# Convolution operations tied in the plan to the pace of the feed-forward items

## The chip, the cores and the metric

The kernel runs on one core of one Trainium2 chip. The metric is the device time of one execution in microseconds (us). Engines are called as in the profile: PE (TensorE), DVE (VectorE), ACT (ScalarE), POOL (GpSimd) and SP (SyncE, which here issues DMA).

## What is computed

A dynamic convolution over 2 x 4096 tokens of width 192, and behind it two feed-forward layers of width 2048, all in float32:

```python
w = softmax(weight_gen)                    # per token and head: 7 taps
x = sum over k of w[..., k] * x_shifted[k] # 8 heads of 24 columns, 6 tokens back
h = x @ w_in1;  g = where(h >= 1, h, where(h <= -1, 0, (h + 1)**2 / 4))
x = g @ w_out1                             # layer 1
h = x @ w_in2;  g = h - tanh(h)
out = g @ w_out2                           # layer 2
```

## The kernel before

The 8192 tokens are cut into 16 blocks of 512. A block goes through the convolution once and through layer 1 (m = 0) and layer 2 (m = 1). In a layer the hidden width of 2048 is 16 slices of 128; one slice of one block in one layer is an **item** (m, b, f). The order of the 512 items is written down in `order`: blocks 0 to 2 at the start in a mixed way, and then in turn 16 items of layer 1 of block b and 16 of layer 2 of block b - 1. Such 32 items are called a cycle here, 16 of them half a cycle. `at` gives an item's place.

An item (`item`) runs in this way. PE multiplies the block's columns with a slice of w_in into a PSUM bank. ACT and DVE make g of it: in layer 1 two ACT steps (L787, L788) and one of DVE (L789), in layer 2 one ACT step (L791) and one of DVE (L792). To keep float32 accuracy, g is split: ACT casts the high part gh (L793), DVE subtracts to get the low part gl (L797). PE multiplies gh and gl with a slice of w_out into two accumulator banks. At the end of a block `finish1` (layer 1, lines 844 to 856) or `finish2` (layer 2: an ACT copy at L877, DVE at L878 to L880, then 24 stores on SP's queue) takes the accumulators away.

From layer 1 of block 4 and layer 2 of block 3 on, two items run as a pair (`both`): matmuls of 64 rows, two at a time on the two halves of the array, 38 to a pair. A pair has three parts: `one` makes most of the first projection of its two items and the rest of the second projection of older ones, `two` reads gh and gl of the later item of the pair before the last, `three` those of the earlier item of the last pair.

The convolution of a block (`conv`) is a softmax of five short DVE steps and one of ACT, then 7 multiplications (L437) and 6 additions (L484, the last of them L573) over 128 x 768 values on DVE. For blocks 4 to 15 `move_rows` then splits the sum into a high and a low part (ACT L574, DVE L576), turns both (DVE L568, twice), sends them to DRAM and reads them back as columns. That makes 16 large DVE operations for a block.

The order of work on each engine is not written by hand. `Plan.add` takes a task with its engines and assumed durations, a key, the tasks that it depends on, and the buffers that it takes. `Plan.run` plays through these durations: whenever an engine is free it starts the ready task with the lowest key. What comes out is one fixed row of instructions for each engine, and only that reaches the chip, where an instruction waits for its data and for the instructions ahead of it in its row. An item's tasks have its place as key. A convolution's tasks begin at `base`, 36 places ahead of its block (40 for block 3), and go up by 1.1; but as they are started whenever nothing with a lower key is ready, they run far ahead of their keys, up to the number of buffers.

Of the kernel before, what the change touches and what calls it, by code (L numbers as in the profile page):

```python
# [14 lines left out]
ALU = mybir.AluOpType  # L15
AX = mybir.AxisListType
# [7 lines left out]
MOVED = 4  # L24
# [133 lines left out]
def on(engine, dur):  # L158
    return {engine: (dur, 0.0)}
# [3 lines left out]
def tile_dynconv_moe_moe(  # L163
# [86 lines left out]
    plan = Plan()  # L250
# [23 lines left out]
    order = []  # L274
# [96 lines left out]
    def conv(b, banks, base, gap):  # L371
# [4 lines left out]
        spare = slot("xt") if early else None  # L376
        j0 = b * T
        n0 = max(0, PAD - j0)
        count = [0]

        def key():
            count[0] += 1
            return base + gap * count[0]

        def load_wg(e):
            e.dma_start(wgs[wg.n].rearrange("p j h k -> p j (h k)"), wg_pj[:, b * T:(b + 1) * T, :])
# [18 lines left out]
        def bc(t):  # L405
            return t.unsqueeze(3).to_broadcast([P, T, H, K])
# [14 lines left out]
        lh = plan.add(on("DMA", 0.42 * n0), base - lead, load_halo, takes=[xw], late=2.0) if n0 else None  # L421
        lx = plan.add(on("DMA", 0.42 * (T + PAD - n0)), base - lead, load_x, takes=[] if n0 else [xw], uses=[xw] if n0 else [], late=2.0)
        whole = lambda k: lh if k + T <= n0 else lx
        t = plan.add(on("DVE", 0.30), key(), lambda e: e.tensor_reduce(MX(), W(), axis=AX.X, op=ALU.max), [lw], takes=soft, uses=[wg], own=0.12 if early else 0.0)
        t = plan.add(on("DVE", 0.30), key(), lambda e: e.tensor_tensor(W(), W(), bc(MX()), op=ALU.subtract), [t], uses=[wg] + soft, lock=not early)
        t = plan.add(on("ACT", 0.30), key(), lambda e: e.activation(W(), W(), AF.Exp), [t], uses=[wg])
        t = plan.add(on("DVE", 0.30), key(), lambda e: e.tensor_reduce(SM(), W(), axis=AX.X, op=ALU.add), [t], uses=[wg] + soft, own=0.12 if early else 0.0)

        def inverse(e):
            e.tensor_scalar(SM(), SM(), 1e-9, None, ALU.add)  # L430
            e.reciprocal(SM(), SM())

        t = plan.add(on("DVE", 0.47), key(), inverse, [t], uses=[wg] + soft, late=0.05, own=0.12 if early else 0.0)
        ts = plan.add(on("DVE", 0.30), key(), lambda e: e.tensor_tensor(W(), W(), bc(SM()), op=ALU.mult), [t], uses=[wg] + soft, lock=not early)

        def tap(e, dst, w, k):
            e.tensor_tensor(  # L437
# [53 lines left out]
        for fn, k, kind in tasks:  # L491
            last = early and k == mine - 1
            t = plan.add(
                on("DVE", 0.87), key(), fn, dep + [whole(k), lh], takes=([] if kind or k else [mem] + (area2 if b == 0 else [])),
                uses=([] if kind else [wg, xw]) + (more if kind or k or b else area) + ([mem] if kind or k else []),
                late=0.1, own=0.12 if early and b and (k if kind == 0 else last) else 0.0, lock=not early,
            )
            dep = [t]
# [5 lines left out]
            dep = [plan.add(on("DVE", 0.87), key(), lambda e: e.tensor_tensor(end, end, pool_mem(0), op=ALU.add), dep + [pa], uses=more + [spare], own=0.12)]  # L504

        if b >= MOVED:
            move_rows(b, wg, xw, mem, xt, dep, key)
            return

        def last_sum(e):  # L510
# [45 lines left out]
        marks["evac", b] = l1  # L556
        xdone[0, b] = [h0, h1, l0, l1]

    def move_rows(b, wg, xw, mem, xt, dep, key):
# [12 lines left out]

        t = plan.add(on("DVE", 0.87), key(), lambda e: e.tensor_tensor(acc_sb, acc_sb, prod_sb, op=ALU.add), dep, uses=[mem], lock=True)  # L573
        th = plan.add(on("ACT", 0.72), key(), lambda e: e.copy(hi_sb, acc_sb), [t], uses=[mem])  # L574
        tq = plan.add(on("DVE", 0.87), key(), lambda e: squares(e, 0, prod_sb), [th], uses=[mem, xw])
        tl = plan.add(on("DVE", 0.87), key(), lambda e: e.tensor_tensor(acc_sb, acc_sb, prod_sb, op=ALU.subtract), [th], uses=[mem], lock=True)  # L576
        tr = plan.add(on("DVE", 0.87), key(), lambda e: squares(e, 1, acc_sb), [tl, tq], uses=[mem, xw])
# [128 lines left out]
    def done(g, t):  # L706

        if g in late2 and late2[g][2] == NF - 1:
            m, b, f, *_, acc, need = late2[g]
            (finish1 if m == 0 else finish2)(b, acc, g + 7.0, t)  # L710

    def both(m, b, f, h0, h1, need):

# [22 lines left out]

        opens = [s for g in (g0, g1) if late2[g][2] == 0 for s in late2[g][8]]
        rest = lambda g: [s for s in used(g) if s not in opens]
        t = plan.add(on("PE", 2.08), i, one, need + [last[0]], takes=[h0, h1], uses=[xs, x3_of[m, b]] + used(o0, o1), late=0.0)
        done(o0, t)  # L740
        mid = plan.add(on("PE", 1.155), i, two, [t] + late2[g0][9], takes=[s for s in opens if s in late2[g0][8]], uses=[h0, xs] + used(o1) + rest(g0), late=0.35)
        done(o1, mid)
        end = last[0] = plan.add(on("PE", 1.155), i + 1, three, [mid] + late2[g1][9], takes=[s for s in opens if s in late2[g1][8]], uses=[h1, xs, x3_of[m, b]] + rest(g1), late=0.35)
        prev2[late2[g1][:2]] = end
        return mid, end

# [13 lines left out]
    def item(m, b, f, after):  # L760
# [178 lines left out]
UNTIL = 3.5  # L939
SKEW = 12  # L940
SKEW2 = 12
BASE3, BASE = 40.0, 36.0
LEAD = (4.0, 6.0)
CONV1 = (0.0, 0.35)
CONV2 = (14.0, 0.6)
# [29 lines left out]
```

## Time and profile before

| | |
|---|---|
| median of 3 runs | 1201.31 us (1200.46 to 1201.41) |
| the profiled execution | 1199.51 us, its span 1197.7 us |
| PE | busy 1151.5 us, 96% of the span |
| DVE | busy 994.1 us, 83% |
| ACT | busy 849.1 us, 71% |
| POOL | busy 98.6 us, 8%, all near the start |

The span is from the first to the last instruction of that one execution. Busy shares are means over stages: the start, with the weights being split into high and low parts, until about 225 us; whole-height items until 295 us; pairs until 1151 us; then the last half block. PE's records overlap, since the end of a matmul is modelled, so a busy PE can still be fed late.

### The profile page before, as it was taken

How to read it: one execution, taken by the hardware profiler on the slowest of the kernel's cores; microseconds unless marked ns; L12 is line 12 of the kernel's file. 1: busy time of each engine (PE TensorE's matmuls, PEld its weight loads, DVE VectorE, ACT ScalarE, POOL GpSimd, SP SyncE). 2: the span in 40 equal slices, each digit the busy share in tenths (PEclk: the TensorE clock that was granted, in tenths of full speed). 3: DMA queues.
4: the chain of work that ended last, by engine and by line, in shares of the span. 5: the costliest groups of instructions: out<-in, count | busy, mean ns of one | idle time of the engine just before them, and what ended most of it. 6: DMA issues, size and time to landing. Idle time of an engine off the chain costs nothing.

```text
span 1197.7 us, 23410 instructions
## 1 busy us (share of the span) xinstructions
PE 1151.5 (96%) x8648; PEld 1034.3 (86%) x8648; DVE 994.1 (83%) x1519; ACT 849.1 (71%) x1511; POOL 98.6 (8%) x85
## 2 busy tenths in 40 slices
PE   3899999999999999999999999999999999999998
PEld 2578778888788898999989899898999999999987
DVE  8999998999999989698796978779666666666665
ACT  4989896675767768677675766757677676867653
POOL 4743650000000000000000000000000000000000
PEclk9999999999999999999999999999999999999999
DMA  7422130232230213003030210302011010100000
GB/s 212 150 70 78 53 119 6 53 83 77 77 95 11 70 34 100 10 15 95 1 108 1 62 47 7 99 1 71 2 18 55 6 41 1 45 1 15 1 9 19
DMA packets 93034, 60.50 MB, mean 51 GB/s; under 512 B 56060, under 2 KB 81274, under 8 KB 92920
## 3 DMA queue, kind: packets, MB, share of 16 engines
q1 hardware_dynamic: 92732, 58.62, 17.4%
q8 instruction: 68, 1.11, 0.4%
q10 hardware_dynamic: 188, 0.39, 0.1%
q14 instruction: 46, 0.38, 0.1%
HBM read 43.24 MB, written 15.73 MB: 49 GB/s over the span
## 4 chain that ended last, share of the span: by engine, by line
PE 76%; DVE 14%; issue 4%; ACT 3%; DMA 2%; POOL 0%; SPq 0%; DVEq 0%; ACTq 0%; POOLq 0%
PE ps L669 33%; PE ps L685 29%; PE ps L773 7%; DVE gl L797 3%; DVE g L789 3%; DVE acc L484 1%; PE ps L814 1%; PE ps L808 1%; DVE prod L437 1%; PE ps L815 1%; PE ps L809 1%; PE ps L810 1%; PE ps L825 1%; DVE g L792 1%; ACT gh L793 1%
## 5 line engine op out<-in xcount | busy, mean ns | idle before, releaser
L669 PE MATMUL ps<-gh,wout 64*128 64x512 f32 x2304 | 730.2, 388 | 0.8 <-ACT gh L793 0.3
L669 PE MATMUL ps<-gl,wout 64*128 64x512 f32 x1536 | 597.2, 390 | 8.2 <-DVE gl L797 7.2
L669 PEld LDWEIGHTS ps<-gh,wout 64*128 64x128 f32 x2304 | 417.9, 184 | 29.2 <-ACT gh L793 8.7
L793 ACT CAST gh<-g 128x512 fp32r<-128x512 f32 x512 | 315.1, 617 | 145.7 <-DVE g L792 54.5
L685 PE MATMUL ps<-a,win 64*128 64x512 f32 x1632 | 413.6, 391 | 0.0
L685 PE MATMUL ps<-b,win 64*128 64x512 f32 x1632 | 403.4, 387 | 0.0
L797 DVE TENSOR_TENSOR gl<-g,gh 128x512 fp32r<-128x512 f32 x474 | 325.9, 691 | 44.9 <-PE ps L669 21.1
L669 PEld LDWEIGHTS ps<-gl,wout 64*128 64x128 f32 x1536 | 282.9, 184 | 26.8 <-DVE gl L797 21.6
L685 PEld LDWEIGHTS ps<-a,win 64*128 64x128 f32 x1632 | 296.5, 184 | 8.3 <-issue 0.4
L685 PEld LDWEIGHTS ps<-b,win 64*128 64x128 f32 x1632 | 299.9, 184 | 3.8
L792 DVE TENSOR_TENSOR g<-ps,g 128x512 f32<-128x512 f32 x256 | 175.2, 687 | 84.9 <-ACT g L791 84.2
L791 ACT ACTIVATE g<-ps 128x512 f32<-128x512 f32 x256 | 152.4, 597 | 110.9 <-PE ps L685 99.4
L789 DVE SCALAR_TENSOR_TENSOR g<-ps,g 128x512 f32<-128x512 f32 x256 | 173.1, 682 | 51.0 <-ACT g L788 50.7
L787 ACT ACTIVATE g<-ps 128x512 f32<-128x512 f32 x256 | 151.2, 591 | 39.8 <-PE ps L685 36.6
L788 ACT ACTIVATE g<-g 128x512 f32<-128x512 f32 x256 | 161.8, 632 | 6.4
L773 PE MATMUL ps<-a,win 128*128 128x512 f32 x320 | 85.8, 402 | 7.6 <-POOL win L351 2.7
L773 PE MATMUL ps<-b,win 128*128 128x512 f32 x320 | 83.7, 392 | 2.3 <-DVE val L331 2.3
L437 DVE TENSOR_TENSOR prod<-xw,wg 128x768 f32<-128x768 f32 x84 | 82.9, 987 | 0.5
L773 PEld LDWEIGHTS ps<-a,win 128*128 128x128 f32 x320 | 60.6, 192 | 25.2 <-POOL win L351 4.0
L685 PE MATMUL ps<-x,win 64*128 64x512 f32 x192 | 74.4, 387 | 0.0
L773 PEld LDWEIGHTS ps<-b,win 128*128 128x128 f32 x320 | 58.8, 188 | 15.4 <-DVE val L331 3.6
L484 DVE TENSOR_TENSOR acc<-acc,prod 128x768 f32<-128x768 f32 x70 | 68.2, 974 | 0.1
(89 smaller groups left out, 894.4 us busy)
## 6 DMA issues: line engine op xcount, KB each, us to landing
xw<-in_x_dram SPq DMA_DIRECT2D x14, 960.0 KB, 4.8
spot<-xw SPq DMA_DIRECT2D x96, 96.0 KB, 2.1
raw<-in_moe_w_out_dram SPq DMA_DIRECT2D x16, 384.0 KB, 3.1
a<-spot SPq DMA_DIRECT2D x24, 256.0 KB, 3.3
out_dram<-raw SPq DMA_DIRECT2D x360, 16.0 KB, 1.5
raw<-in_moe_w_in_dram SPq DMA_DIRECT2D x16, 256.0 KB, 3.0
raw<-in_moe_w_in_dram SPq DMA_DIRECT2D x32, 128.0 KB, 3.2
a<-spot SPq DMA_DIRECT2D x24, 128.0 KB, 3.1
```

Of the source, the lines that this page charges most:

```text
L437: e.tensor_tensor(dst.rearrange("p j (h g) -> p j h g", h=H), xws[xw.n][:, k:k + T, :].rearrange("p j (h g) -> p j h g", h=H), w[:, :, :, ...
L484: e.tensor_tensor(prods[k % 2] if early and k == mine - 1 else acc_sb, acc_sb, prods[k % 2], op=ALU.add)
L669: return e.matmul(to(), w[rs, c:c + P], (GL() if low else GH())[rs], start=f == 0 and lane == 0 and n == 0, stop=f == NF - 1 and lane == 1 ...
L685: return e.matmul(ps[h.n], win[m][rs, k, fs], x, start=lane == 0 and n == 0, stop=lane == 1 and n == len(ops) - 1)
L773: e.matmul(ps[h.n], w[:, k, fs], xt[:, c], start=n == 0, stop=n == 4)
L787: t = plan.add(on("ACT", 0.60), i, lambda e: e.activation(G_(), H_(), AF.Relu, bias=0.5, scale=0.5), [first], takes=[g], uses=[h], late=0.1)
L788: t = plan.add(on("ACT", 0.537), i, lambda e: e.activation(G_(), G_(), AF.Square), [t], uses=[g])
L789: t = plan.add(on("DVE", 0.605), i, lambda e: e.scalar_tensor_tensor(G_(), H_(), 1.0, G_(), op0=ALU.max, op1=ALU.min), [t], uses=[g, h])
L791: t = plan.add(on("ACT", 0.49), i, lambda e: e.activation(G_(), H_(), AF.Tanh), [first], takes=[g], uses=[h])
L792: t = plan.add(on("DVE", 0.605), i, lambda e: e.tensor_tensor(G_(), H_(), G_(), op=ALU.subtract), [t], uses=[g, h])
L793: thi = plan.add(on("ACT", 0.527), i, lambda e: e.copy(GH(), G_()), [t], takes=[gh], uses=[g])
L797: tlo = plan.add(engines, i, lambda e: e.tensor_tensor(GL(), G_(), GH().bitcast(F32), op=ALU.subtract), [thi], takes=[gl], uses=[g], lock= ...
```

## The change

Tasks of `conv` for blocks 4 to 15 on DVE get one more dependency, from the new function `turn`. It counts the operations (short ones as 0.5, large ones as 1) and returns the gl task of the item that stands 1.3 places further on for each; places count from `base`, which moves from 36 to 40 places ahead of the block. The dependency is one of the plan: the instruction itself has no use for that gl. The tasks at the end of a paired block get the key of the item plus 9 (layer 1) or plus 11 (layer 2) instead of plus 7, and the planner's durations of the three parts of a pair are 1 to 2% shorter.

```diff
+        def turn(k):
+
+            if b < MOVED:
+                return []
+            paced[0] += k
+            n = int(base + PACE * paced[0])
+            return [marks["gl", it] for it in [order[n]] if n < at[0, b, 0] and ("gl", it) in marks]
...
-        t = plan.add(on("DVE", 0.30), key(), lambda e: e.tensor_reduce(MX(), W(), axis=AX.X, op=ALU.max), [lw], takes=soft, uses=[wg], own=0.12 if early else 0.0)
+        t = plan.add(on("DVE", 0.30), key(), lambda e: e.tensor_reduce(MX(), W(), axis=AX.X, op=ALU.max), [lw] + turn(0.5), takes=soft, uses=[wg], own=0.12 if early else 0.0)
...
-                on("DVE", 0.87), key(), fn, dep + [whole(k), lh], takes=([] if kind or k else [mem] + (area2 if b == 0 else [])),
+                on("DVE", 0.87), key(), fn, dep + [whole(k), lh] + turn(1.0), takes=([] if kind or k else [mem] + (area2 if b == 0 else [])),
...
-            (finish1 if m == 0 else finish2)(b, acc, g + 7.0, t)
+            (finish1 if m == 0 else finish2)(b, acc, g + (9.0 if m == 0 else 11.0), t)
...
-        t = plan.add(on("PE", 2.08), i, one, need + [last[0]], takes=[h0, h1], uses=[xs, x3_of[m, b]] + used(o0, o1), late=0.0)
+        t = plan.add(on("PE", 2.045), i, one, need + [last[0]], takes=[h0, h1], uses=[xs, x3_of[m, b]] + used(o0, o1), late=0.0)
...
+        marks["gl", (m, b, f)] = tlo
...
-BASE3, BASE = 40.0, 36.0
+BASE3, BASE = 40.0, 40.0
+PACE = 1.3
```

The other short steps of the softmax and the four DVE operations of `move_rows` get `turn(0.5)` and `turn(1.0)` in the same way; parts `two` and `three` of a pair go from 1.155 to 1.135. The numbers of the lines behind `turn` go up by 8, from the line after gl by 9.

On DVE, in layer 1 of a middle block, the row before has this piece; L797 is gl, L789 is g, L437, L484 and L573 are operations of a convolution:

```order
L797 TENSOR_TENSOR gl_105<-g_95,gh_100 128x512
L437 TENSOR_TENSOR prod_94<-xw_91,wg_77 128x768
L797 TENSOR_TENSOR gl_103<-g_96,gh_99 128x512
L484 TENSOR_TENSOR acc_93<-acc_93,prod_94 128x768
L789 SCALAR_TENSOR_TENSOR g_97<-ps_65,g_97 128x512
L437 TENSOR_TENSOR prod_94<-xw_91,wg_77 128x768
L797 TENSOR_TENSOR gl_104<-g_97,gh_98 128x512
L789 SCALAR_TENSOR_TENSOR g_95<-ps_66,g_95 128x512
L484 TENSOR_TENSOR acc_93<-acc_93,prod_94 128x768
L437 TENSOR_TENSOR prod_94<-xw_91,wg_77 128x768
L797 TENSOR_TENSOR gl_102<-g_95,gh_101 128x512
```

The same place on DVE in the row after (L805 is gl, L797 is g, L445 and L492 the convolution's):

```order
L797 SCALAR_TENSOR_TENSOR g_97<-ps_66,g_97 128x512
L797 SCALAR_TENSOR_TENSOR g_95<-ps_65,g_95 128x512
L805 TENSOR_TENSOR gl_102<-g_97,gh_101 128x512
L492 TENSOR_TENSOR acc_93<-acc_93,prod_94 128x768
L805 TENSOR_TENSOR gl_104<-g_95,gh_98 128x512
L797 SCALAR_TENSOR_TENSOR g_96<-ps_67,g_96 128x512
L797 SCALAR_TENSOR_TENSOR g_97<-ps_68,g_97 128x512
L805 TENSOR_TENSOR gl_103<-g_96,gh_99 128x512
L445 TENSOR_TENSOR prod_94<-xw_92,wg_78 128x768
L805 TENSOR_TENSOR gl_105<-g_97,gh_100 128x512
L492 TENSOR_TENSOR acc_93<-acc_93,prod_94 128x768
```

There the convolution's operations were up to three to a pair of items, and now are one or two, each behind a gl.

The end of a layer 2 block on DVE, which falls into layer 1 of the next cycle, in the row before (L878 to L880 are `finish2`):

```order
L789 SCALAR_TENSOR_TENSOR g_97<-ps_66,g_97 128x512
L797 TENSOR_TENSOR gl_104<-g_96,gh_98 128x512
L878 STREAM_TRANSPOSE raw_85<-ps_64 128x512
L879 TENSOR_TENSOR val_89<-ps_64,val_89 64x512
L797 TENSOR_TENSOR gl_102<-g_97,gh_101 128x512
L789 SCALAR_TENSOR_TENSOR g_95<-ps_67,g_95 128x512
L880 STREAM_TRANSPOSE raw_85<-val_89 64x512
```

and the same place on DVE in the row after (L887 to L889):

```order
L797 SCALAR_TENSOR_TENSOR g_97<-ps_65,g_97 128x512
L887 STREAM_TRANSPOSE raw_85<-ps_64 128x512
L805 TENSOR_TENSOR gl_102<-g_96,gh_101 128x512
L805 TENSOR_TENSOR gl_104<-g_97,gh_98 128x512
L445 TENSOR_TENSOR prod_94<-xw_92,wg_78 128x768
L797 SCALAR_TENSOR_TENSOR g_95<-ps_67,g_95 128x512
L888 TENSOR_TENSOR val_89<-ps_64,val_89 64x512
L889 STREAM_TRANSPOSE raw_85<-val_89 64x512
L805 TENSOR_TENSOR gl_103<-g_95,gh_99 128x512
```

The first of the three moved from behind the pair's first gl to a place ahead of it, the other two to behind the first g of the next pair.

Near the start, on DVE, the last steps of the second layer's weights (L326 and L331; 128x512 belongs to w_in, 128x384 to w_out) in the row before:

```order
L792 TENSOR_TENSOR g_96<-ps_68,g_96 128x512
L326 SCALAR_TENSOR_TENSOR ps_66<-ps_66,raw_86 128x384
L792 TENSOR_TENSOR g_97<-ps_65,g_97 128x512
L331 SCALAR_TENSOR_TENSOR val_89<-raw_86,ps_66 128x384
L797 TENSOR_TENSOR gl_102<-g_96,gh_101 128x512
L792 TENSOR_TENSOR g_95<-ps_67,g_95 128x512
L351 TENSOR_TENSOR wout_84<-val_89,wout_84 128x2x128
L351 TENSOR_TENSOR wout_84<-val_89,wout_84 128x2x64
L326 SCALAR_TENSOR_TENSOR ps_65<-ps_65,raw_87 128x512
L797 TENSOR_TENSOR gl_105<-g_97,gh_100 128x512
L331 SCALAR_TENSOR_TENSOR val_90<-raw_87,ps_65 128x512
```

and on DVE in the row after:

```order
L331 SCALAR_TENSOR_TENSOR val_89<-raw_86,ps_66 128x384
L800 TENSOR_TENSOR g_95<-ps_67,g_95 128x512
L800 TENSOR_TENSOR g_96<-ps_68,g_96 128x512
L800 TENSOR_TENSOR g_97<-ps_65,g_97 128x512
L326 SCALAR_TENSOR_TENSOR ps_66<-ps_66,raw_87 128x512
L805 TENSOR_TENSOR gl_102<-g_95,gh_101 128x512
L331 SCALAR_TENSOR_TENSOR val_90<-raw_87,ps_66 128x512
```

The sign step of the last piece of w_in (val_90 from raw_87) stood behind 62 operations that make g and stands behind 64 now.

## Rows read from the trace of the kernel before

**Rows 1.** The page: span, busy time of PE, granted clock in 40 slices

```profile
span 1197.7 us, 23410 instructions
PE 1151.5 (96%) x8648; PEld 1034.3 (86%) x8648; DVE 994.1 (83%) x1519; ACT 849.1 (71%) x1511; POOL 98.6 (8%) x85
...
PEclk9999999999999999999999999999999999999999
```

**Rows 2.** Busy time by stretches of 304 matmuls: start:end, length, engines

```profile
core 0: us, PE busy (x) PEld busy (x) DVE busy (x) ACT busy (x) POOL busy (x), PEclk, DMA share, GB/s
294.94:332.66 37.72, 36.29 (x295) 30.18 (x296) 37.51 (x57) 27.90 (x48) 0.00 (x0) 1.00 0.24 62
332.66:369.07 36.41, 36.22 (x308) 30.43 (x305) 36.24 (x58) 23.74 (x41) 0.00 (x0) 1.00 0.26 78
369.07:406.51 37.44, 36.41 (x308) 30.36 (x305) 37.27 (x58) 28.80 (x50) 0.00 (x0) 1.00 0.09 15
406.51:441.25 34.74, 34.74 (x307) 31.57 (x304) 30.87 (x55) 22.98 (x41) 0.00 (x0) 1.00 0.27 82
441.25:477.84 36.59, 35.97 (x307) 31.29 (x306) 36.30 (x57) 28.34 (x50) 0.00 (x0) 1.00 0.27 68
...
512.43:549.82 37.39, 36.26 (x308) 32.21 (x306) 36.68 (x57) 28.24 (x50) 0.00 (x0) 1.00 0.29 77
...
800.41:837.80 37.39, 36.26 (x307) 32.21 (x306) 35.35 (x51) 27.98 (x49) 0.00 (x0) 1.00 0.23 58
837.80:872.40 34.60, 34.60 (x307) 33.98 (x305) 23.41 (x36) 21.81 (x38) 0.00 (x0) 1.00 0.01 1
```

**Rows 3.** DVE in order of time: start, length, what; last large convolution operation

```profile
831.05 0.97 DVE L568 STREAM_TRANSPOSE xw<-acc 128x768 f32<-128x768 f32 x1
```

**Rows 4.** Waits of PE, 294 to 1152 us: total, times, longest

```profile
PE ps L669 <- DVE gl L797: 7.2, 14, 0.8
```

**Rows 5.** DVE in order of time, in a crowded half cycle

```profile
610.33 0.69 DVE L797 TENSOR_TENSOR gl<-g,gh 128x512 fp32r<-128x512 f32 x1
610.93 0.68 DVE L789 SCALAR_TENSOR_TENSOR g<-ps,g 128x512 f32<-128x512 f32 x1
611.53 0.97 DVE L568 STREAM_TRANSPOSE xw<-prod 128x768 f32<-128x768 f32 x1
612.42 0.92 DVE L576 TENSOR_TENSOR acc<-acc,prod 128x768 f32<-128x768 f32 x1
613.26 0.68 DVE L797 TENSOR_TENSOR gl<-g,gh 128x512 fp32r<-128x512 f32 x1
```

**Rows 6.** DVE in order of time, end of a layer 2 block

```profile
597.21 0.71 DVE L878 STREAM_TRANSPOSE raw<-ps 128x512 f32<-128x512 f32 x1
597.84 0.64 DVE L879 TENSOR_TENSOR val<-ps,val 64x512 f32<-64x512 f32 x1
```

**Rows 7.** DVE in order of time, an undisturbed pair of layer 1

```profile
907.40 0.69 DVE L789 SCALAR_TENSOR_TENSOR g<-ps,g 128x512 f32<-128x512 f32 x1 [1.05 <-ACT g L788]
908.55 0.69 DVE L789 SCALAR_TENSOR_TENSOR g<-ps,g 128x512 f32<-128x512 f32 x1 [0.46 <-ACT g L788]
909.16 1.52 DVE L797 TENSOR_TENSOR gl<-g,gh 128x512 fp32r<-128x512 f32 x2
```

**Rows 8.** PE in order of time: readers of those two gl

```profile
910.62 0.39 PE L669 MATMUL ps<-gl,wout 64*128 64x512 f32 x1
...
913.79 0.39 PE L669 MATMUL ps<-gl,wout 64*128 64x512 f32 x1
```

**Rows 9.** ACT in order of time, the pair's later cast

```profile
909.33 0.62 ACT L793 CAST gh<-g 128x512 fp32r<-128x512 f32 x1 [0.30 <-DVE g L789]
```

**Rows 10.** The page: DMA issues, KB each, us to landing

```profile
a<-spot SPq DMA_DIRECT2D x24, 256.0 KB, 3.3
```

**Rows 11.** Busy time in a stretch near the start

```profile
140.00:165.00 25.00, 22.10 (x94) 17.03 (x93) 24.53 (x40) 21.90 (x44) 11.51 (x10) 1.00 0.32 100
```

**Rows 12.** Waits of PE, 80 to 296 us

```profile
PE ps L773 <- DVE val L331: 2.3, 2, 1.6
```

More of the change, by code (lines that the diff above doesn't have):

```diff
@@ L378, in conv @@
         n0 = max(0, PAD - j0)
-        count = [0]
+        count, paced = [0], [0.0]
         def key():
@@ L423, in conv @@
         whole = lambda k: lh if k + T <= n0 else lx
-        t = plan.add(on("DVE", 0.30), key(), lambda e: e.tensor_reduce(MX(), W(), axis=AX.X, op=ALU.max), [lw], takes=soft, uses=[wg], own=0.12 if early else 0.0)
-        t = plan.add(on("DVE", 0.30), key(), lambda e: e.tensor_tensor(W(), W(), bc(MX()), op=ALU.subtract), [t], uses=[wg] + soft, lock=not early)
+        t = plan.add(on("DVE", 0.30), key(), lambda e: e.tensor_reduce(MX(), W(), axis=AX.X, op=ALU.max), [lw] + turn(0.5), takes=soft, uses=[wg], own=0.12 if early else 0.0)
+        t = plan.add(on("DVE", 0.30), key(), lambda e: e.tensor_tensor(W(), W(), bc(MX()), op=ALU.subtract), [t] + turn(0.5), uses=[wg] + soft, lock=not early)
         t = plan.add(on("ACT", 0.30), key(), lambda e: e.activation(W(), W(), AF.Exp), [t], uses=[wg])
-        t = plan.add(on("DVE", 0.30), key(), lambda e: e.tensor_reduce(SM(), W(), axis=AX.X, op=ALU.add), [t], uses=[wg] + soft, own=0.12 if early else 0.0)
+        t = plan.add(on("DVE", 0.30), key(), lambda e: e.tensor_reduce(SM(), W(), axis=AX.X, op=ALU.add), [t] + turn(0.5), uses=[wg] + soft, own=0.12 if early else 0.0)
         def inverse(e):
@@ L431, in inverse @@
             e.reciprocal(SM(), SM())
-        t = plan.add(on("DVE", 0.47), key(), inverse, [t], uses=[wg] + soft, late=0.05, own=0.12 if early else 0.0)
-        ts = plan.add(on("DVE", 0.30), key(), lambda e: e.tensor_tensor(W(), W(), bc(SM()), op=ALU.mult), [t], uses=[wg] + soft, lock=not early)
+        t = plan.add(on("DVE", 0.47), key(), inverse, [t] + turn(0.5), uses=[wg] + soft, late=0.05, own=0.12 if early else 0.0)
+        ts = plan.add(on("DVE", 0.30), key(), lambda e: e.tensor_tensor(W(), W(), bc(SM()), op=ALU.mult), [t] + turn(0.5), uses=[wg] + soft, lock=not early)
         def tap(e, dst, w, k):
@@ L506, in conv @@
         if b >= MOVED:
-            move_rows(b, wg, xw, mem, xt, dep, key)
+            move_rows(b, wg, xw, mem, xt, dep, key, turn)
             return
@@ L557, in conv, with move_rows @@
         xdone[0, b] = [h0, h1, l0, l1]
-    def move_rows(b, wg, xw, mem, xt, dep, key):
+    def move_rows(b, wg, xw, mem, xt, dep, key, turn):
         Q = P // 32
@@ L571, in squares @@
             )
-        t = plan.add(on("DVE", 0.87), key(), lambda e: e.tensor_tensor(acc_sb, acc_sb, prod_sb, op=ALU.add), dep, uses=[mem], lock=True)
+        t = plan.add(on("DVE", 0.87), key(), lambda e: e.tensor_tensor(acc_sb, acc_sb, prod_sb, op=ALU.add), dep + turn(1.0), uses=[mem], lock=True)
         th = plan.add(on("ACT", 0.72), key(), lambda e: e.copy(hi_sb, acc_sb), [t], uses=[mem])
-        tq = plan.add(on("DVE", 0.87), key(), lambda e: squares(e, 0, prod_sb), [th], uses=[mem, xw])
-        tl = plan.add(on("DVE", 0.87), key(), lambda e: e.tensor_tensor(acc_sb, acc_sb, prod_sb, op=ALU.subtract), [th], uses=[mem], lock=True)
-        tr = plan.add(on("DVE", 0.87), key(), lambda e: squares(e, 1, acc_sb), [tl, tq], uses=[mem, xw])
+        tq = plan.add(on("DVE", 0.87), key(), lambda e: squares(e, 0, prod_sb), [th] + turn(1.0), uses=[mem, xw])
+        tl = plan.add(on("DVE", 0.87), key(), lambda e: e.tensor_tensor(acc_sb, acc_sb, prod_sb, op=ALU.subtract), [th] + turn(1.0), uses=[mem], lock=True)
+        tr = plan.add(on("DVE", 0.87), key(), lambda e: squares(e, 1, acc_sb), [tl, tq] + turn(1.0), uses=[mem, xw])
         last = key()
@@ L738, in both @@
         rest = lambda g: [s for s in used(g) if s not in opens]
-        t = plan.add(on("PE", 2.08), i, one, need + [last[0]], takes=[h0, h1], uses=[xs, x3_of[m, b]] + used(o0, o1), late=0.0)
+        t = plan.add(on("PE", 2.045), i, one, need + [last[0]], takes=[h0, h1], uses=[xs, x3_of[m, b]] + used(o0, o1), late=0.0)
         done(o0, t)
-        mid = plan.add(on("PE", 1.155), i, two, [t] + late2[g0][9], takes=[s for s in opens if s in late2[g0][8]], uses=[h0, xs] + used(o1) + rest(g0), late=0.35)
+        mid = plan.add(on("PE", 1.135), i, two, [t] + late2[g0][9], takes=[s for s in opens if s in late2[g0][8]], uses=[h0, xs] + used(o1) + rest(g0), late=0.35)
         done(o1, mid)
-        end = last[0] = plan.add(on("PE", 1.155), i + 1, three, [mid] + late2[g1][9], takes=[s for s in opens if s in late2[g1][8]], uses=[h1, xs, x3_of[m, b]] + rest(g1), late=0.35)
+        end = last[0] = plan.add(on("PE", 1.135), i + 1, three, [mid] + late2[g1][9], takes=[s for s in opens if s in late2[g1][8]], uses=[h1, xs, x3_of[m, b]] + rest(g1), late=0.35)
         prev2[late2[g1][:2]] = end
```

## Prediction, made blind

> **What bounds the kernel now.** I read the page first, then the stretches. The span is 1197.7 us and PE is called busy for 96% of it [rows 1], so whatever can be won is time in which PE is fed late. The clock slices are all 9 [rows 1]: the granted clock is at its upper level throughout and gives nothing back. "Busy" hides small gaps, because matmul ends are modelled and overlap, so I compare equal amounts of PE work instead. From 294.94 us on, blocks run in pairs of items. A pair is 38 matmuls, and half a cycle of blocks (16 items, 8 pairs) is 304 of them. The stretches cut at those points [rows 2] show two kinds. With no convolution work on VectorE (837.80; the last large convolution operation starts at 831.05 [rows 3], and the half cycles after it repeat this row) half a cycle takes 34.60 us, which is 4.325 us a pair; VectorE is busy for 23.4 of it. That is the floor. Where convolution work falls in, the same work takes 37.4 us (512.43 and 800.41, the first and the last of five alike, 72 us apart), with VectorE busy for 35 to 37 us. The excess over 34.60 is 3.1, 1.8, 2.8, 0.1 and 2.0 us in the five stretches from 294.94 to 477.84, and 2.8 us in each of the five alike: 9.8 + 14.1 = **23.9 us**. PE's waits name the cause: matmuls of the second projection on gl, 14 times, 7.2 us [rows 4]. That is only the part that the modelled ends leave visible.
>
> Why VectorE is late there: it runs back to back, each instruction starting before the record of the one ahead ends. A g or gl takes a step of 0.60 us, a large convolution operation 0.84 to 0.89, taken as 0.87, an operation at the end of a block about 0.6 [rows 5, 6]. A pair needs two g and two gl, 2.42 us, so 1.9 us of its 4.325 are free: room for two convolution operations (1.74), not for three. In the order before, the 16 large operations of one block, and three of a block end, stand among 25 g and gl (the piece of the order shown ahead is from this). Their work is 16 x 0.87 + 3 x 0.6 + 25 x 0.605 = 30.8 us, while 25 g and gl are 6.25 pairs, 27.0 us of PE. VectorE falls 3.8 us behind; the slack of the pipeline swallows about 1, and 2.8 are paid. The arithmetic gives the measured excess, so I trust it for the order after.
>
> **The change part by part.** No instruction of the steady stretches is added or removed. The new entries in the dependency lists exist for the planner alone: they fix where an operation stands in VectorE's row, and at run time it still waits only for its data.
>
> (1) Pacing. In the order after, the same 16 + 3 operations of a block stand among 40 g and gl, two to a pair at most. Work 13.9 + 1.8 + 40 x 0.605 = 39.9 us against 10 pairs, 43.2 us of PE. VectorE then has 3.3 us to spare per block instead of lacking 3.8. Left alone this takes away the whole 23.9 us. The ahead-running goes too: before, VectorE has finished its last convolution at 832 us [rows 3]; after, it carries one block's convolution in every cycle until block 15. So eleven cycles (blocks 5 to 15) have convolution work, not five full and some partial ones, and what one costs counts eleven times.
>
> (2) What one still costs, by a walk along the row with these steps. Undisturbed, the first g of a pair has 1.05 us of idle before it, the second 0.46, and the first gl ends at 909.84, 0.78 us before PE reads it at 910.62 [rows 7, 8]. That 0.7 or so is the slack of the early item; the later item's gl ends at 910.68 and is read in the middle of the next pair, some 3 us later. "A, g, g, gl, M, gl" (A an add, M a multiplication): A fits in the 1.05; M stands between the two gl, makes the second late by 0.66, harmless, and the next g by 0.39 if another A follows, which the next idle gives back. The hard place is the end of the other stream's block. The transpose of line 878 stands between the second g and the first gl of pair 2, and two more end operations behind the next pair's first g. There the first gl is late by 0.6 to 0.9 (the upper end if the transpose must wait 0.25 us for PE's last matmul), the next one by 0.2 to 0.4, and the third, because g (1.2 late), ACT's cast of 0.62 [rows 9] and gl follow each other, by 0.8. Over a slack of 0.7 this costs PE 0.1 to 0.4 us, then "g, g, gl, A, gl", 3.3 us, recovers. I take 0.3: 11 x 0.3 = **3.3 us given back**. Its bounds: 0 if the slack covers all, 1.0 if each of the three places overshoots by a third of a step.
>
> (3) Later block ends (+9 and +11 instead of +7). Three VectorE operations, one ACT copy and the 24 stores behind them come a pair or so later. Who waits: the accumulator banks, next used some 30 items on, and SP's queue, in which the load of the weights of a later convolution now stands behind those stores, again about half a cycle early. The end of the convolution (away to DRAM, back) falls some 13 items, 28 us, before its block begins; the transfers back land in 3.3 us [rows 10]. Cost 0; without that cover, one landing, 3 us a block.
>
> (4) Durations of PE in the planner (2.045 and 1.135) and BASE 40: they shift keys only; costed inside (1).
>
> (5) The start. The order also differs from about 90 to 225 us, where the weights of the second layer are prepared. From 140 to 165 us PE issues 94 matmuls [rows 11]; a full-height matmul takes the time of two half-height ones, 4.325 / 19 = 0.228 us, so they are 21.4 us of the 25. VectorE is busy for 24.5 of them, and PE waits 2.3 us for the weights' sign step [rows 12]. For: up to the 64th g VectorE has ten small convolution operations fewer (about 4 us). Against: the sign step of the last first-projection chunk stands behind 64 g instead of 62, closer to its use. The two act on the same wait, so I take **0**, with -4 (all of that excess gone) to +4 (as much again).
>
> Sum against the profiled execution's own time, 1199.51 us (1.8 over its span): 1199.5 - 23.9 + 3.3 + 0 = 1178.9. The median of the runs, 1201.31, lies 1.8 above it, so the forecast is 1180.7, say **1181 us**.
>
> **The rivals.** (a) Half of the stalls stay: the walk misses something in every cycle (ACT's casts shifted by the copy to the low part, the transposes waiting for PE), and a cycle costs 1 to 2 us. 1201.3 - 23.9 + 11 x 1.5 = 1194 us, 1188 to 1199. For it: 13 of the 16 large operations still stand in the half with the heavier ACT chain. Against: no pair there carries more than two, and the walk already holds that chain. (b) Slower: VectorE in that half is as short as today, since pairs with a block end do need 4.8 to 5.4 us of the 4.325, and each of eleven cycles pays today's 2.8 us: 1201.3 - 23.9 + 30.8 = 1208 us. It decides from 23.9 / 11 = 2.2 us a cycle. Against it: today's 2.8 comes from six overfull pairs nearly in a row, here there are two, and pairs of 3.3 and 4.2 us follow. (c) The stalls are not VectorE's work at all but a ring of buffers that is too short; the order then leaves them where they are, 1201 us, give or take 2. The Trainium skill (Perfetto Trace Analysis, Optimization Strategy) reads the same gap recurring on the engine that should be full as possibly too few buffers for the next tile. By that rule the 23.9 us would stay; by the rows they go. The rows speak against it: the same buffers serve the undisturbed halves at 34.60 us [rows 2], and the wait is on gl being written [rows 4]. (d) The planner's start is the bad part: four more us with (1) as forecast, 1185 us.
>
> **How the numbers follow.** Forecast, with (d) as its upper part: 0.73. (a) 0.15, (b) 0.07, (c) 0.05. A measurement of this kernel can tell about 0.2%, 2.4 us, from no change. Faster by more: the forecast and nearly all of (a), 0.88. Within 0.2%: (c) and a rest of (a), 0.05. Slower: (b), 0.07. The forecast's own range is 1174 (nothing left per cycle, 3 us won at the start) to 1188; to hold 8 in 10 the range takes in the middle of (a): 1174 to 1194.
>
> **What would show it.** Right: cut at the same matmul counts, all 24 half cycles take 34.6 to 35.0 us, those after 840 us included; VectorE's busy time in a cycle is alike from 300 to 1040 us and no longer above 36 of 37 us anywhere; PE's waits on gl fall from 7.2 to under 2 us, and what is left stands at the third to fifth pair of a half with a block end. The last convolution operation moves from about 830 to beyond 1000 us. (5) is read at the point where the paired stretch begins, now 294.94 us. Wrong: half cycles of 36 us and more all the way, (a) or (b); gaps where VectorE is idle, (c) or a late DMA.

## The result, and the profile after the change

The changed kernel takes 1182.52 us in the median of five runs (1182.21 to 1182.92); the kernel before, timed beside it, 1201.41 (1200.46 to 1201.72). The ratio is 0.9844, with an interval of 0.9829 to 0.9858: faster by 1.6%. The forecast was 1181 us, the range 1174 to 1194. The profiled execution after the change took 1182.38 us (span 1180.6), the one before 1199.51 (span 1197.7): 17.1 us less, by either measure of the two traces.

The page of the kernel after, its span, busy times and granted clock, answering to [rows 1]:

```profile
span 1180.6 us, 23472 instructions
PE 1144.8 (97%) x8648; PEld 1027.2 (87%) x8648; DVE 995.9 (84%) x1523; ACT 849.1 (72%) x1511; POOL 94.0 (8%) x81
...
PEclk9899999999999999999999999999999999999999
```

The matmuls are as many as before. The granted clock is at its upper level (2.4 GHz) in all slices but the second, where the mean of this one execution is 0.88:

```profile
29.50:59.00 29.50, 25.61 (x98) 19.51 (x97) 29.15 (x49) 27.00 (x57) 20.91 (x19) 0.88 0.51 161
```

That costs nothing by the end of the slice: the 121st matmul starts at 58.78 us after the change and at 58.84 before it. So the difference is again time in which PE is fed late. Cut at the same counts of matmuls as [rows 2] (start:end, length, then PE, PEld, DVE, ACT, POOL busy, granted clock, DMA share, GB/s), the kernel after reads:

```profile
290.38:325.94 35.56, 35.30 (x295) 32.27 (x296) 30.22 (x44) 26.66 (x46) 0.00 (x0) 1.00 0.09 16
325.94:360.61 34.67, 34.67 (x306) 33.99 (x305) 28.55 (x46) 22.49 (x40) 0.00 (x0) 1.00 0.26 78
...
641.68:677.23 35.55, 35.27 (x307) 30.61 (x305) 31.85 (x47) 27.84 (x48) 0.00 (x0) 1.00 0.09 16
677.23:711.90 34.67, 34.67 (x308) 28.68 (x305) 28.58 (x46) 22.45 (x40) 0.00 (x0) 1.00 0.27 79
...
992.62:1028.15 35.53, 35.25 (x307) 32.57 (x305) 31.85 (x47) 27.74 (x48) 0.00 (x0) 1.00 0.08 12
1062.81:1097.48 34.67, 34.67 (x306) 33.99 (x305) 22.88 (x35) 27.57 (x48) 0.00 (x0) 1.00 0.08 13
```

The half cycles of 37.4 us are gone. Up to the last convolution VectorE carries 28 to 32 us of work in every half cycle instead of 35 to 37 in some and 23 in others. But there are now two kinds that take turns: the half with layer 1 of a block loses 0.8 to 1.2 us (mostly 0.87), eleven times, and the half with layer 2 loses nothing. The last large convolution operation, which started at 831.05 us in [rows 3], starts at 1034.74 us.

PE's waits in the paired stretch (total us, times, longest), answering to [rows 4], kernel after, 290 to 1135 us:

```profile
PE ps L677 <- DVE gl L805: 3.1, 11, 0.3
```

Still the same wait, once a cycle, 3.1 us instead of 7.2. The start of the kernel, 140 to 165 us, answering to [rows 11]:

```profile
140.00:165.00 25.00, 25.00 (x112) 20.71 (x111) 23.71 (x35) 23.48 (x50) 17.20 (x15) 1.00 0.35 111
```

PE issues 112 matmuls there instead of 94, and of the wait for the weights' sign step in [rows 12] nothing is left. The paired stretch begins at 290.38 us instead of 294.94.

The account between the two profiled executions:

| Part | Us |
|---|---|
| start, up to the first pair (294.94 to 290.38) | -4.6 |
| stalls of the order before, as predicted | -23.9 |
| new stalls, 11 half cycles | +9.75 |
| floor 34.67 instead of 34.60 us, 24 half cycles | +1.6 |
| behind the pairs (46.3 us in both) | 0 |
| sum | -17.1 |

**Where the new stall is.** The pair lengths in a layer 1 half cycle, counted from the matmul at 641.68 us, are 4.33, 4.33, 4.95, 4.34, 4.57, 4.36, 4.33, 4.33 us: 0.62 us lost in the third pair and 0.24 in the fifth. VectorE, ScalarE and PE at the third pair, kernel after, each in order of time (start, length, engine, what, and in brackets the idle time ahead and who ended it):

```profile
651.16 1.43 DVE L797 SCALAR_TENSOR_TENSOR g<-ps,g 128x512 f32<-128x512 f32 x2
653.15 0.72 DVE L887 STREAM_TRANSPOSE raw<-ps 128x512 f32<-128x512 f32 x1 [0.56 <-ACT val L886]
653.78 1.25 DVE L805 TENSOR_TENSOR gl<-g,gh 128x512 fp32r<-128x512 f32 x2
```

```profile
651.88 0.62 ACT L801 CAST gh<-g 128x512 fp32r<-128x512 f32 x1
652.53 0.58 ACT L886 COPY val<-ps 64x512 f32<-64x512 f32 x1
```

```profile
651.99 0.39 PE L677 MATMUL ps<-gl,wout 64*128 64x512 f32 x1
...
653.82 0.39 PE L693 MATMUL ps<-a,win 64*128 64x512 f32 x1
654.49 0.49 PE L677 MATMUL ps<-gl,wout 64*128 64x512 f32 x1 [0.28 <-DVE gl L805]
```

The block end's transpose (L887) stands ahead of the pair's two gl. It sits at the head of VectorE's row until ScalarE's copy of the same block end (L886) is through, 0.56 us with VectorE idle. ScalarE in turn reaches that copy only behind a cast. PE isn't what the transpose waits for: PE's last matmul of that block is the one at 651.99 us, and its record ends at 652.38, before VectorE is done with the two g. The gl behind the transpose come late, and PE stops.

### The profile page after: what moved, and what is told of

Its sections match the earlier page's. It is cut to its first block, busy times and chain, and to the rows that moved or that the text cites. A ratio compares the mean times of both kernels' runs of the same rounds, so it can differ in the third digit from the quotient of the medians.

```text
span 1180.6 us, 23472 instructions
## 1 busy us (share of the span) xinstructions
PE 1144.8 (97%) x8648; PEld 1027.2 (87%) x8648; DVE 995.9 (84%) x1523; ACT 849.1 (72%) x1511; POOL 94.0 (8%) x81
## 4 chain that ended last, share of the span: by engine, by line
PE 87%; ACT 6%; DVE 4%; issue 1%; POOL 1%; DMA 1%; DVEq 0%; ACTq 0%
PE ps L677 36%; PE ps L693 31%; PE ps L781 10%; PE ps L823 2%; PE ps L824 2%; PE ps L817 2%; PE ps L818 2%; PE ps L819 2%; ACT g L795 1%; ACT g L796 1%; ACT gh L801 1%; PE ps L834 1%; DVE gl L805 1%; DVE raw L887 1%; ACT val L886 1%
## 5 line engine op out<-in xcount | busy, mean ns | idle before, releaser
L693 PE MATMUL ps<-a,win 64*128 64x512 f32 x1632 | 408.7, 389 | 0.0
L805 DVE TENSOR_TENSOR gl<-g,gh 128x512 fp32r<-128x512 f32 x476 | 327.5, 692 | 41.4 <-ACT gh L801 26.2
L797 DVE SCALAR_TENSOR_TENSOR g<-ps,g 128x512 f32<-128x512 f32 x256 | 174.6, 685 | 47.5 <-ACT g L796 44.8
L445 DVE TENSOR_TENSOR prod<-xw,wg 128x768 f32<-128x768 f32 x84 | 80.9, 963 | 0.0
L492 DVE TENSOR_TENSOR acc<-acc,prod 128x768 f32<-128x768 f32 x70 | 67.4, 963 | 0.0
```

The costliest lines, as they stand in the source:

```text
L445: e.tensor_tensor(dst.rearrange("p j (h g) -> p j h g", h=H), xws[xw.n][:, k:k + T, :].rearrange("p j (h g) -> p j h g", h=H), w[:, :, :, ...
L492: e.tensor_tensor(prods[k % 2] if early and k == mine - 1 else acc_sb, acc_sb, prods[k % 2], op=ALU.add)
L693: return e.matmul(ps[h.n], win[m][rs, k, fs], x, start=lane == 0 and n == 0, stop=lane == 1 and n == len(ops) - 1)
L797: t = plan.add(on("DVE", 0.605), i, lambda e: e.scalar_tensor_tensor(G_(), H_(), 1.0, G_(), op0=ALU.max, op1=ALU.min), [t], uses=[g, h])
```

## The experiments

Two questions: which part of the change is worth what, and whether the 0.62 us is the place of the transpose, the wait for ScalarE, or something else. The theory was at first the prediction's own, VectorE's row, and the rivals are named with each run. Ratios are against the kernel before, timed beside each run (medians of 1199.86 to 1200.43 us).

Some parts needed no run. With the block-end keys put back to +7, or moved on to +14, the changed kernel has instruction for instruction the same order on PE, VectorE, ScalarE and SyncE. The keys alone, or BASE 40 alone without the pacing, leave the kernel before as it was. So the order follows from the pacing and the planner's durations, and the later block ends of the diff move nothing. (With the planner's old durations they do: there, keys of +7 put the second transpose of a middle block end one gl and one g earlier.)

### The planner's durations alone

```diff
-            if b < MOVED:
+            if True:
...
-            (finish1 if m == 0 else finish2)(b, acc, g + (9.0 if m == 0 else 11.0), t)
+            (finish1 if m == 0 else finish2)(b, acc, g + (7.0 if m == 0 else 7.0), t)
...
-BASE3, BASE = 40.0, 40.0
+BASE3, BASE = 40.0, 36.0
```

> Of the change only the planner's shorter durations of PE (2.045 and 1.135) stay; pacing, BASE 40 and the later block ends are undone. On VectorE the 16 large convolution operations and the three of a block end of a middle block then stand among 26 g and gl (25 before, 40 with pacing). Theory 1 (what counts is how many convolution operations stand to a pair of items): work 13.9 + 1.8 + 26 x 0.605 = 31.4 us against 6.5 pairs, 28.1 us; half cycles with convolution work stay at 36.5 to 37.5 us, the start is as before (pairs from 294.9 us), the time is 1196 to 1202 us. Rival (the durations alone bring the better order): under 1190 us.

Measured: 1196.57 us, ratio 0.9968 (0.9957 to 0.998). A middle half cycle of it:

```profile
656.68:693.03 36.35, 35.58 (x308) 32.05 (x305) 34.98 (x51) 27.79 (x48) 0.00 (x0) 1.00 0.26 62
```

VectorE is still crowded (35 us), the half cycle still loses 1.7 us, PE's waits on gl are 8.2 us. Its pairs begin at 296.26 us, 1.3 us later than before and not at the same time, as was expected. The durations by themselves are worth 0.3%; the pacing is what makes the change.

### The change without the new durations

```diff
-        t = plan.add(on("PE", 2.045), i, one, need + [last[0]], takes=[h0, h1], uses=[xs, x3_of[m, b]] + used(o0, o1), late=0.0)
+        t = plan.add(on("PE", 2.08), i, one, need + [last[0]], takes=[h0, h1], uses=[xs, x3_of[m, b]] + used(o0, o1), late=0.0)
...
```

(and 1.155 for 1.135 in the two other parts of a pair)

> The changed kernel with the planner's old durations of PE (2.08 and 1.155). Pacing, BASE and keys stay. The transpose of a block end then stands behind the first gl of its pair instead of ahead of it, and the two other end operations stand in two different pairs. Theory 1 (the 0.62 and 0.23 us that a cycle of the changed kernel still loses come from the end operations ahead of a gl): a half cycle of layer 1 takes 34.7 to 34.9 us instead of 35.5, the time is 1173 to 1177 us. Rival (they come from two convolution operations to a pair, wherever the block end stands): 35.5 us stays, 1181 to 1184 us.

Measured: 1172.01 us, ratio 0.9765 (0.9752 to 0.9778), below what was expected.

```profile
983.49:1018.12 34.63, 34.63 (x307) 33.95 (x305) 31.62 (x47) 27.73 (x48) 0.00 (x0) 1.00 0.08 13
```

The same 31.6 us of VectorE work, and no stall at all. Its block end on VectorE, kernel without the new durations:

```profile
648.11 0.69 DVE L805 TENSOR_TENSOR gl<-g,gh 128x512 fp32r<-128x512 f32 x1
648.72 0.72 DVE L887 STREAM_TRANSPOSE raw<-ps 128x512 f32<-128x512 f32 x1
```

and ScalarE's copy:

```profile
648.10 0.59 ACT L886 COPY val<-ps 64x512 f32<-64x512 f32 x1
```

The transpose stands behind the first gl again and VectorE has no idle time ahead of it: the copy ends some 0.03 us before it starts. So inside the change the durations cost 0.8% (0.9844 against 0.9765): with shorter pairs the planner reckons with the block's last matmul earlier, and puts the transpose one place ahead of the gl.

### Pacing from block 6 on only

```diff
-            if b < MOVED:
+            if b < 6:
```

> The changed kernel, but blocks 4 and 5 aren't paced (as in the kernel before); blocks 6 to 15 are. Theory 1 (the 4.6 us that the changed kernel wins ahead of the paired stretch come from the convolution operations of blocks 4 and 5 that no longer stand between the steps of the weights): pairs begin at 294 to 296 us as before, PE's waits on the weights' sign step are back (about 2 us), the first half cycles cost 1 to 3 us more, the time is 1187 to 1192 us. Rival (the start is won by something else, or by chance of the order): pairs begin at 290 to 292 us, 1182 to 1186 us.

Measured: 1186.29 us, ratio 0.9882 (0.9868 to 0.9895). Waits of PE from 80 to 296 us, and two half cycles:

```profile
PE ps L781 <- DVE val L331: 2.3, 2, 1.5
```

```profile
295.08:329.63 34.55, 34.55 (x295) 32.99 (x296) 21.43 (x33) 26.62 (x46) 0.00 (x0) 1.00 0.17 39
364.08:399.63 35.55, 35.16 (x307) 30.99 (x306) 31.92 (x47) 27.79 (x48) 0.00 (x0) 1.00 0.09 16
```

The wait for the sign step is back and the pairs begin at 295.08 us, as before: the gain of the start, 4.7 us here, comes from the paced convolutions of blocks 4 and 5. The other half of what was expected missed, and the time lies just under the expected 1187 us. The unpaced early blocks cost the first half cycles nothing (34.55 and 34.45 us), where 1 to 3 us had been allowed; the first of them even lacks the stall that it has in the change (35.56 us).

### BASE 36 in the change

```diff
-BASE3, BASE = 40.0, 40.0
+BASE3, BASE = 40.0, 36.0
```

> The changed kernel with BASE at 36 again; pacing, durations and keys stay. The convolution begins four items later, so that its operations stand in other pairs, and the transpose of the block end still stands behind the second g and ahead of the first gl of its pair, followed by an add in the next pair. Theory 1 (the loss of a cycle is the transpose ahead of the gl): the loss stays at 0.6 to 1.2 us, 1180 to 1186 us. Rival (where the convolution stands decides, the block end doesn't matter): a loss under 0.3 us or over 1.5 us a cycle, under 1177 or over 1189 us.

Measured: 1182.75 us, ratio 0.9851 (0.9834 to 0.9867), no difference from the change that can be measured. The transpose waits as it did, in the kernel with BASE 36:

```profile
652.94 0.72 DVE L887 STREAM_TRANSPOSE raw<-ps 128x512 f32<-128x512 f32 x1 [0.56 <-ACT val L886]
```

Starting the convolutions four places later moves the crowd, not the loss. The loss belongs to the block end.

### The transpose behind the first gl

```diff
-        t0 = plan.add(on("DVE", 0.60), key, lambda e: e.transpose(R()[:, 0:N], p0()), [t], takes=[s], uses=acc)
+        z = at[1, b, NF - 1]
+        back = [marks.get(("gl", order[z + 3]))] if z + 3 < len(order) and paired(1, b) else []
+        t0 = plan.add(on("DVE", 0.60), key, lambda e: e.transpose(R()[:, 0:N], p0()), [t] + back, takes=[s], uses=acc)
```

> The changed kernel with one more dependency in the plan: the first transpose of a layer 2 block end waits for the first gl of its pair, so that it stands behind it. All else stays: pacing, new durations, BASE 40. Theory 1 (the 0.62 us stall is the transpose, held by ACT's copy, ahead of that gl; the 0.23 us one follows from it): both are gone or under 0.1 us, the time is 1170 to 1175 us, as with the old durations. Rival (the other end operations and the convolution make them): at least 0.4 us a cycle stays, 1177 us or more.

Measured: 1173.96 us, ratio 0.9774 (0.976 to 0.9789), with the durations of the change kept.

```profile
638.01:672.64 34.63, 34.63 (x308) 33.94 (x306) 31.63 (x47) 27.72 (x48) 0.00 (x0) 1.00 0.09 16
```

The half cycles run at 34.61 to 34.68 us; only the first stays at 35.54, the end of block 3, which the edit does not reach. So the order of the block end is the change's whole loss. It isn't one operation alone, though. The edit names the first transpose, but the planner then moves the second one too: after the change it stands right behind the add and ahead of the next pair's first gl, here behind two more gl and the two g of the pair after that.

```profile
657.51 0.69 DVE L891 STREAM_TRANSPOSE raw<-val 64x512 f32<-64x512 f32 x1
658.14 1.24 DVE L805 TENSOR_TENSOR gl<-g,gh 128x512 fp32r<-128x512 f32 x2
```

Which of the two moves takes away the 0.24 us of the fifth pair this run can't tell.

### The copy behind the transpose

The transpose keeps its place ahead of the gl, but is planned ahead of ScalarE's copy:

```diff
-        h1 = plan.add(on("ACT", 0.60), key, lambda e: e.copy(M(), p1()[D1:P]), [t], takes=[tm], uses=acc)
         t0 = plan.add(on("DVE", 0.60), key, lambda e: e.transpose(R()[:, 0:N], p0()), [t], takes=[s], uses=acc)
+        h1 = plan.add(on("ACT", 0.60), key, lambda e: e.copy(M(), p1()[D1:P]), [t0] if paired(1, b) else [t], takes=[tm], uses=acc)
```

> The changed kernel with ACT's copy at a layer 2 block end planned behind the transpose instead of ahead of it. VectorE's row is the same, the transpose still stands ahead of the first gl; only what it waits for on ACT changes. Theory 1 (in the changed kernel the transpose starts 0.55 us late because it is released by the end of ACT's copy): it starts up to 0.5 us earlier, the first stall falls from 0.62 to 0.1 to 0.3 us, but the copy ends later and the next end operation with it; 1176 to 1181 us. Rival (the place ahead of the gl is what costs, whatever it waits for): 0.5 us or more, 1181 to 1184 us.

Measured: 1176.46 us, ratio 0.9795 (0.9781 to 0.981). The order on VectorE is that of the change in all cycles but the last. The block end there, with the copy behind:

```profile
648.21 1.42 DVE L797 SCALAR_TENSOR_TENSOR g<-ps,g 128x512 f32<-128x512 f32 x2
649.54 0.71 DVE L886 STREAM_TRANSPOSE raw<-ps 128x512 f32<-128x512 f32 x1
650.17 1.25 DVE L805 TENSOR_TENSOR gl<-g,gh 128x512 fp32r<-128x512 f32 x2
...
652.87 0.67 DVE L888 TENSOR_TENSOR val<-ps,val 64x512 f32<-64x512 f32 x1
653.58 0.70 DVE L889 STREAM_TRANSPOSE raw<-val 64x512 f32<-64x512 f32 x1
654.21 0.64 DVE L805 TENSOR_TENSOR gl<-g,gh 128x512 fp32r<-128x512 f32 x1
```

and the half cycle around it:

```profile
638.70:673.63 34.93, 34.93 (x307) 33.06 (x305) 31.83 (x47) 27.72 (x48) 0.00 (x0) 1.00 0.09 16
```

The transpose starts right behind the two g, with no idle time. The third pair loses 0.02 us instead of 0.62, the fifth still 0.29, in all 0.3 a cycle (34.93 us against 34.62 in the half cycle behind it). So the places alone cost 0.3, and the rest of 0.87 was the wait for the copy. The loss of the fifth pair doesn't follow from that of the third, as had been thought: it stays when the other is gone, with the add and the second transpose still ahead of a gl.

The traces also show where the wait comes from. In the kernel after, 14 of the 15 first transposes carry a wait on a semaphore that only ScalarE's instructions raise; with the copy behind, 13 of 15 carry one that only PE's matmuls raise, and 11 of the copies one that VectorE's raise. So the program orders the two readers of the block's accumulators, whichever is planned first, and the wait is no delay that the chip adds. Both accumulators of a block lie in one PSUM tile (`ps_64` in the orders shown ahead); whether that is the reason was not tested.

### More room: convolutions 56 and 58 places ahead

```diff
-                conv(b, (2, 3), at[0, b, 0] - (BASE3 if b == 3 else BASE), 1.1)
+                conv(b, (2, 3), at[0, b, 0] - (40.0 if b < 5 else 56.0), 1.1)
```

> The changed kernel with the convolutions of blocks 5 to 15 begun 56 places ahead of their block instead of 40 (block 4 stays at 40). Twelve of the 16 large operations then fall into the half cycle of layer 2, whose ACT chain is shorter, the others ahead of it, and none stands near the end of a layer 2 block. Theory 1 (what a cycle still loses is the meeting of the convolution with the block end in layer 1): all half cycles take 34.6 to 34.8 us, the time is 1172 to 1176 us, lower than the changed kernel's 1182.5. Rival (the loss comes from pacing as such, two large operations to a pair): a cycle loses 0.9 us as now, only in the other half, 1181 to 1184 us.

Measured: 1167.67 us (1166.79 to 1169.05), ratio 0.973 (0.9717 to 0.9743). No stall is left, and a half cycle takes 34.45 us, below the 34.60 that the prediction called the floor:

```profile
635.06:669.51 34.45, 34.45 (x306) 33.43 (x306) 27.41 (x46) 28.14 (x50) 0.00 (x0) 1.00 0.34 91
```

In this kernel the first transpose of a block end stands behind the first gl of its pair, the add and the second transpose behind the second gl. Of its 14.8 us against the change (spans 1180.6 and 1165.8), 9.75 are the stalls and about 24 x 0.22 = 5.3 the lower floor. Is the floor a matter of the stalls, or of the number 56? Block 9 alone put back to 40:

```diff
-                conv(b, (2, 3), at[0, b, 0] - (BASE3 if b == 3 else BASE), 1.1)
+                conv(b, (2, 3), at[0, b, 0] - (40.0 if b < 5 or b == 9 else 56.0), 1.1)
```

> The kernel with the convolutions 56 places ahead, but block 9 alone at 40: one cycle of the whole run in which the convolution meets the block end. It is to tell where the pair of 4.306 us (half cycles of 34.45) comes from that the kernel at 56 has all the way, while every other kernel here has 4.325 to 4.334 (34.60 to 34.67). Theory A (how the two rows of half-height matmuls are interleaved in time is set when PE last stood still, and stays): 34.45 up to the first stall, then 34.5 to 34.7 in all half cycles to the end, though none of them has a stall. Rival B (the slower pair comes from VectorE or ACT work beside it, or from the chip of that run): 34.45 again as soon as that cycle is over.

Measured, one run: 1175.26 us.

```profile
533.42:568.08 34.66, 34.66 (x306) 33.98 (x305) 26.20 (x43) 21.99 (x39) 0.00 (x0) 1.00 0.01 1
568.08:603.61 35.53, 35.25 (x306) 31.74 (x305) 32.71 (x53) 27.85 (x49) 0.00 (x0) 1.00 0.09 16
```

Block 9 brings its stall back, as it should. The half cycle behind it loses more, 1.4 us, for the end of one convolution and the start of the next meet there and three large operations stand in a row:

```profile
603.61:639.70 36.09, 35.29 (x307) 30.61 (x305) 35.88 (x52) 22.34 (x39) 0.00 (x0) 1.00 0.27 79
```

But the half cycles are 34.66 us ahead of block 9 too, from the first ones on. Neither expectation fits: that stall did not set the floor. So the kernel with 56 ran once more, on another chip:

> The kernel with the convolutions 56 places ahead once more, unchanged, to see whether its pair of 4.306 us (34.45 us a half cycle) is a property of the kernel or a state that an execution falls into when the paired stretch begins. Theory A (a state set by the last small hold-up of PE; without hold-ups it stays to the end): the profile shows one and the same half cycle from about 330 us to the end, either 34.45 or one of 34.60 and 34.67, and the times of the rounds lie in groups some 4 us apart, between 1166 and 1173 us. Rival B (the kernel's own): 34.45 us again, all rounds within 1166 to 1169 us.

Measured: 1170.51 us, ratio 0.9754 (0.974 to 0.9768). It is the same program, and PE waits for no gl in the paired stretch, but now:

```profile
637.48:672.14 34.66, 34.66 (x307) 34.04 (x305) 27.46 (x46) 28.06 (x50) 0.00 (x0) 1.00 0.34 91
```

Rival B is refuted. Of theory A the one length all the way came true (34.63 to 34.67 us), the two groups of times did not: the runs took 1168.13, 1169.68, 1171.34 and 1172.94 us. Then 58 instead of 56, on that second chip:

> As that kernel, with the convolutions of blocks 5 to 15 begun 58 places ahead instead of 56: another order on VectorE, again with the block end behind the first gl of its pair and no more than two large operations to a pair. Theory 1 (what costs is only the crowding and the block end ahead of a gl): no cycle loses more than 0.2 us, half cycles of 34.45 to 34.70 by the state of the two rows of matmuls, 1166 to 1173 us. Rival (56 is a lucky place): a loss of 0.5 us a cycle or more, 1175 us or more.

Measured: 1168.35 us (1168.06 to 1168.57), ratio 0.9735 (0.9722 to 0.9749), half cycles of 34.45 us:

```profile
636.09:670.54 34.45, 34.45 (x307) 33.42 (x306) 27.34 (x45) 28.00 (x49) 0.00 (x0) 1.00 0.33 80
```

So the order does not fix the floor, since one program showed both; nor does the chip alone, since the first one gave 34.45 (56) and 34.66 (block 9 at 40), the second 34.66 (56) and 34.45 (58). That an order can favour one of them isn't excluded: each run has the profile of one execution. All these orders (56 twice, 58) are 2.5 to 2.7% faster than the kernel before, and faster than the change. Over the change without the new durations (0.9765) their lead of 0.1 to 0.35% can be the floor alone.

## Why the prediction came out right, and which steps did not

**What bounds it: right.** The 23.9 us of stalls were VectorE's crowded row. The paced order carries the same work and they are gone, in the change and, with nothing left over, in three experiments. Rival (c), buffers that are too short, is refuted: the same buffers serve 34.45 to 34.66 us once the order is another. The Trainium skill's reading of a recurring gap as possibly too few buffers (Perfetto Trace Analysis, Optimization Strategy) would have left the time at 1201 us; the measured 1182.5 decides against it here. Rival (b) needed 2.2 us a cycle and found 0.87. That lies just under the 1 to 2 us of rival (a): 0.87 instead of its 1.5 would have given 1187 us, and the start paid 4.6 of that back.

**(1) Pacing, -23.9: right in size**, the account above is built on it.

**(2) What a cycle still costs: mis-sized.** The walk found the right place, the transpose ahead of the first gl of the third pair (its pair 2), and a late gl behind it, which the runs show in the fifth pair. It gave 0.3 us; the chip took 0.87, so 9.75 us instead of 3.3, inside the bounds of 0 to 1.0 of a typical cycle. The failed step is one clause: "if the transpose must wait 0.25 us for PE's last matmul". It waited 0.56 us, and for ScalarE's copy, which is in the order of ScalarE behind a cast. The walk went down VectorE's row alone and took ScalarE's part in the block end as harmless. With that wait removed the chip gives 0.3 us, what the walk had given.

**(3) Later block ends, 0: right, for a reason not seen.** Beside the new durations the new keys move no instruction. What moved the transpose was (4).

**(4) The durations: costed inside (1), and wrongly seen as neutral.** They move the transpose ahead of the gl, and cost 0.8% inside the change; alone on the kernel before they win 0.3%.

**(5) The start, taken as 0 between -4 and +4: it was -4.6**, just beyond the lower bound. Of the two opposite effects the one for it won: with blocks 4 and 5 unpaced the gain is gone, so it comes from their convolution operations, which no longer stand ahead of the weights' steps. The wait for the sign step vanished, though that step stands two g later.

**The floor.** 34.60 us was taken as fixed. It was 34.67 in the execution after, 1.6 us in all.

**The sum.** +6.5 for (2), -4.6 for (5) and +1.6 for the floor make 3.5 us more than forecast between the profiled executions (1182.4 against 1178.9). Adding 1.8 us for the distance of median and profiled run hid half of that: after the change the two agree (1182.52 and 1182.38). The median lies 1.5 us from the forecast partly by luck. Of the signs named ahead, the fall of VectorE's busy time, the late end of the convolutions and the place of the remaining stall came true. Missed were "all half cycles 34.6 to 35.0 us" (13 of the 24 do) and "waits on gl under 2 us" (3.1).

## What to carry to other kernels

In an in-order row, spread work that has time over the items that have room, and look at what it stands ahead of: here the short operations of a block end, one of them waiting, ahead of the critical one cost 0.87 us a cycle, while 13 large ones placed behind it cost nothing. Before pricing a moved operation, follow its inputs onto the other engines' rows, since a wait at the head of a row is paid by all that is queued behind it. And look at which edits of a plan move an instruction at all: the keys in this diff moved none, while a 2% change of a duration in the planner decided where the costly one stood.

## What the runs showed of the hardware that was not expected

Two streams of half-height matmuls share TensorE in a pair, and how they interleave is not fixed. In the 34.45 us executions (56 in its first run, and 58) matmuls start alternately 57 and 170 ns apart, steadily, and a pair takes 4.306 us. PE in order of time, the first run with 56:

```profile
640.10 0.39 PE L693 MATMUL ps<-a,win 64*128 64x512 f32 x1
640.27 0.39 PE L677 MATMUL ps<-gh,wout 64*128 64x512 f32 x1
640.33 0.39 PE L693 MATMUL ps<-a,win 64*128 64x512 f32 x1
640.50 0.39 PE L677 MATMUL ps<-gl,wout 64*128 64x512 f32 x1
```

and the second run of the same kernel, 34.66 us a half cycle:

```profile
638.69 0.39 PE L677 MATMUL ps<-gl,wout 64*128 64x512 f32 x1
638.84 0.39 PE L693 MATMUL ps<-a,win 64*128 64x512 f32 x1
638.91 0.39 PE L677 MATMUL ps<-gh,wout 64*128 64x512 f32 x1
639.07 0.39 PE L693 MATMUL ps<-a,win 64*128 64x512 f32 x1
```

Here the starts are some 77 and 150 ns apart, and a pair takes 4.333 us. The kernel before has the same two gaps and takes 4.327 us; the kernel after, at 4.333 us, has 63 and 164, 50 and 177 mixed with 57 and 170, or 4 and 223 in different stretches. In all of them the two gaps add up to 227 ns, the step of the whole-height matmuls too (226.7 ns each in the kernel before, from 246 to 290 us), and 19 x 226.7 ns are 4.306 us. The other 20 to 27 ns of the longer pairs are slips of some ns each in the middle part of a pair. The granted clock was 1.00 in all of these stretches. The spacing lasts through the undisturbed pairs, changed at a stall in the run paced from block 6 on (34.45 us a half cycle up to it, 34.6 after), and differs between executions of one kernel. What sets it stays open; it is worth 0.2 us in 34.5, or 5 us of this kernel, more than some of the terms that the prediction worked out.
